# Attention on one core: weights left unnormalized, the reciprocal carried through a transpose into the output

## The chip, the cores and the metric

The kernel runs on one core of a Trainium2 chip. The metric is the device time of one execution in microseconds (us), the median of three runs. Engines are named as in the profile: PE (TensorE matmuls; PEld its weight loads), DVE (VectorE), ACT (ScalarE), POOL (GpSimd), SP (SyncE, which issues the DMAs; SPq is its queue).

## The reference

Rotary attention with 4 x 8 heads, 576 positions and a head size of 64, then two feed-forward layers over 2304 tokens (512 to 2048 to 512). All is float32 for the caller.

```python
q_rot, k_rot = rotate(q), rotate(k)                      # cos/sin tables
scores = matmul(q_rot, k_rot.T) / sqrt(64)
attn = exp(scores - max(scores))
attn = attn / (sum(attn) + 1e-9)
x = matmul(attn, v)                                      # (2304, 512) after the heads are joined
h = x @ w_in;  g = where(h > 0, h, exp(min(h, 0)) - 1);  x = g @ w_out      # layer 1
h = x @ w2_in; g = h - tanh(h);                          out = g @ w2_out   # layer 2
```

## The kernel before

**Attention.** Heads are worked in 16 pairs. The 576 queries of a pair are cut into five blocks; with both heads that makes nine items a pair: items 0 to 7 are four blocks of 128 queries for head 0 and head 1 in turn, item 8 holds the last 64 queries of both heads. One iteration of the loop at L377 is called a *round* here, and a round of a pair is numbered r = 0 to 8 like its item. In round i the kernel records, in this order:

- DMA loads (SP), then the row maximum of item i (`emit_max`, DVE, L216);
- `flush` (L256): the copies out of PSUM of what was transposed in the round before (two of five on DVE at L260, three on ACT at L262), and the attention output: ACT rounds it to the fp32r high part `xh` (L273), and one flush later DVE writes the low part `xl` (L265);
- the scores of item i+1 (`emit_s`, PE, L207), whose PSUM tile has two buffers, so that scores i+1 wait for the exponential of item i-1;
- the exponential of item i (ACT, L230), which also sums the row into `den`;
- `emit_norm` of the block that ended with item i-1: DVE adds 1e-9 to the two columns of sums (L242) and takes reciprocals (L243), POOL multiplies the 128x576 weights of each head by them in place (L246);
- a step of `prep` for a coming pair, by the table at L339 to L349: two multiplications by the cos/sin tables (POOL, L142), an addition (DVE, L144), the high part (ACT, L147), the low part `hl` (DVE, L152) and behind it, in `place`, the DMAs that put high and low part into the q tiles (L177) and k tiles (L174). For k these stand in r = 2, 3, 4 and the k tiles are first read by the scores of the next pair in r = 8;
- in the first sixteen pairs a fifth of the conversion of a layer-1 weight block from raw 64-bit words (`conv_w`; L78 and L79 on DVE in r = 5 of the even pairs);
- the transposes of item i-D with D = 4 (PE, L293; the 64 left-over columns of both heads together at L307), and the products with v (PE, L325) by the table PV_AT: for a group of 256 queries six matmuls in one round and four two rounds later, there with the ten of the last 64 queries in every second case; the trace shows a float32 product as two instructions.

**Layers.** Then come 192 steps of 24 or 21 matmuls each (L442, L498, L500), in which PE reads `xh` and `xl`; layer 1 sums into `acc`, and at its end `acc` is split into high and low part again (L522, L523).

The order on each engine is the order of recording (`manual_schedule`); engines run in order and wait on semaphores.

Of the kernel before, what the change touches and what calls it, by code (L numbers as in the profile page):

```python
# [23 lines left out]
def attention_elu_tanhshrink(ctx: ExitStack, tc: tile.TileContext, qk, v, w1i, w1o, w2i, w2o, tab, out):  # L24
# [76 lines left out]
    with ExitStack() as actx:  # L101
# [9 lines left out]
        ident = acst.tile([128, 128], F32, name="ident")  # L111
        tabs = acst.tile([128, 2, S], F32, name="tabs")
        zero = acst.tile([128, 64], F32, name="zero")
        qa_t = [acst.tile([128, 640], F32R, name=f"qa{i}") for i in range(2)]
# [4 lines left out]
        def load_qk(p, x):  # L119
            if p == 1 and x == 0:  # L120
                t = p3.tile([128, 2, S], F32, tag="a", name="t0")
            else:
                t = (p1, p2)[x].tile([128, 2, S], F32, tag=f"t{x}", name=f"t{x}")
            nc.sync.dma_start(out=t, in_=qk[p, :, 2 * x:2 * x + 2, :])
            t_t[p, x] = t
# [6 lines left out]
        def prep(p, x, i):  # L132
            t = t_t[p, x]
            mul = SCALE if p > 0 and x == 0 else 1.0
            if i < 2:
                if p == 0 and x == 0:
                    nc.vector.scalar_tensor_tensor(
                        out=t[:, i, :], in0=t[:, i, :], scalar=SCALE, in1=tabs[:, i, :], op0=ALU.mult, op1=ALU.mult
                    )
                else:  # L140
                    eng = nc.vector if p < 2 and i == 1 else nc.gpsimd
                    eng.tensor_tensor(out=t[:, i, :], in0=t[:, i, :], in1=tabs[:, i, :], op=ALU.mult)  # L142
            elif i == 2:
                nc.vector.tensor_tensor(out=t[:, 0, :], in0=t[:, 0, :], in1=t[:, 1, :], op=ALU.add)  # L144
            elif i == 3:
                hl_t[p, x] = p1.tile([128, 2, S], F32R, tag=f"hl{x}", name=f"hl{x}")
                nc.scalar.mul(hl_t[p, x][:, 0, :], t[:, 0, :], mul)  # L147
            else:
                hl = hl_t.pop((p, x))
                if p > 0:  # L150
                    t_t.pop((p, x))
                nc.vector.scalar_tensor_tensor(  # L152
                    out=hl[:, 1, :], in0=t[:, 0, :], scalar=mul, in1=hl[:, 0, :].bitcast(F32),
                    op0=ALU.mult, op1=ALU.subtract,
                )
# [78 lines left out]

        def emit_norm(i):
# [13 lines left out]

        ev = [0]  # L250
        late, late_x, late_l = [], [], []

# [3 lines left out]
        def flush():  # L256
# [6 lines left out]
            late.clear()  # L263
            for x0, hp, o, n in late_l:
                nc.vector.tensor_tensor(  # L265
                    out=xl[:, hp, x0:x0 + n], in0=o[:, 0:n], in1=xh[:, hp, x0:x0 + n].bitcast(F32),
                    op=ALU.subtract,
                )
            late_l.clear()
            for p, grp, o, n in late_x:  # L270
                b, hp = divmod(p, 4)
                x0 = b * S + 256 * grp
                nc.scalar.copy(out=xh[:, hp, x0:x0 + n], in_=o[:, 0:n])  # L273
                late_l.append((x0, hp, o, n))
            late_x.clear()

        def emit_t(i):
# [3 lines left out]
            if (u % 2 == 0) and h in (0, None):  # L281
                if grp < 2:
                    aT_t[p, grp] = (p2.tile([128, 2, 4, 256], F32, tag="aT", name="aT"),
                                    p2.tile([128, 256], F32, tag="aTr", name="aTr"))
                else:
                    aT_t[p, grp] = (p1.tile([128, 2, 4, 64], F32, tag="aT2", name="aT2"),
                                    p1.tile([128, 64], F32, tag="aTr2", name="aTr2"))
            aT, aTr = aT_t[p, grp]
# [5 lines left out]
            if h is None:  # L294
                for hh in range(2):
                    evac(aT[:, hh, :, 0:64], pt[:, :, 64 * hh:64 * hh + 64])
                pr = ps_t.tile([128, 4, 128], F32, tag="pt", name="pr")
                for hh in range(2):
                    sl = slice(64 * hh, 64 * hh + 64)
                    nc.tensor.matmul(out=pr[sl, 0, 0:64], lhsT=a[sl, 0, 512:576], rhs=ident[sl, sl],  # L300
                                     start=True, stop=True)
                evac(aTr[:, 0:64], pr[:, 0, 0:64])
                return
            evac(aT[:, h, :, q0:q0 + 128], pt)
            if h == 1:
                pr = ps_t.tile([128, 4, 128], F32, tag="pt", name="pr")
                nc.tensor.transpose(pr[:, 0, :], a.rearrange("p h s -> p (h s)")[:, 512:640], ident)  # L307
                evac(aTr[:, q0:q0 + 128], pr[:, 0, :])

        o_t = {}  # L310

        def emit_pv(p, grp, c):
# [6 lines left out]
            for h in range(2):  # L319
# [10 lines left out]
            if grp == 2:  # L330
                v_t.pop(p)
            late_x.append((p, grp, o, n))
# [6 lines left out]
        early = {1: ((None, 0, 0, 1, 2, 3), (None, 0, 0, 0, 1, 2)), 2: ((2, 4, 5, 7, 7, 8), (4, 7, 9, 11, 12, 13))}  # L339
        for p in range(1, NPAIR):  # L340
            i0 = NI * (p - 1)
            for x in range(2):
                when = [i0 + o for o in ((-8, -6, -4, -3, -2, -1), (-7, -2, 0, 2, 3, 4))[x]]
                if p in early:
# [6 lines left out]
        with tc.manual_schedule():  # L351
            for x in range(2):
                t = t_t[0, x] = (p1, p2)[x].tile([128, 2, S], F32, tag=f"t{x}", name=f"t{x}")
                for i in range(2):
# [3 lines left out]
            load_qk(1, 0)  # L358
            load_qk(1, 1)
            load_v(0)  # L360
            make_identity(nc, ident)
# [8 lines left out]
            n = len(items)  # L370
            pend = []
            emit_s(0)
            PV_AT = ((1, 1, 1, 3, 3), (1, 1, 1, 3, 3), (2, 2, 2, 2, 2))
# [3 lines left out]
            for i in range(n + D + 1):  # L377
                p, r = divmod(i, NI)
                for f, *arg in sched.get(i, ()):
                    if f is not prep:  # L380
                        f(*arg)
                if r == 0 and p % 2 == 0 and p // 2 < len(first_w):
                    load_w(first_w[p // 2])
                if i < n:
# [6 lines left out]
                if 0 <= i - 1 < n:  # L391
                    emit_norm(i - 1)
                if p < NPAIR:
# [19 lines left out]
            flush()  # L413


# [9 lines left out]

    acc = fcst.tile([128, KC * NTOK], F32, name="acc")
    b1 = fcst.tile([128, 1], F32, name="b1")
# [5 lines left out]
    def emit_f1(i):  # L433
# [4 lines left out]
        for c in range(KC):  # L438
            ws = slice(128 * c, 128 * c + 128)
            xs = slice(NB * t, NB * t + NB)  # L440
            for wp, x in ((0, xh), (0, xl), (1, xh)):
                nc.tensor.matmul(out=hp, lhsT=w[:, wp, ws], rhs=x[:, c, xs], start=(m == 0), stop=(m == 3 * KC - 1))  # L442
                m += 1
# [61 lines left out]
    def emit_acc():  # L505
        while y_done:
            l, g, t, ys = y_done.pop()
            for e, y in enumerate(ys):
# [11 lines left out]
                if l == 0:  # L520
                    xs = slice(NB * t, NB * t + NB)
                    nc.scalar.copy(out=xh[:, e, xs], in_=a)  # L522
                    nc.gpsimd.tensor_tensor(  # L523
                        out=xl[:, e, xs], in0=a, in1=xh[:, e, xs].bitcast(F32), op=ALU.subtract
                    )
                else:
# [6 lines left out]
    with tc.manual_schedule():  # L533
# [82 lines left out]
```

## Time and profile before

| | us |
|---|---|
| runs | 1137.78, 1138.52, 1139.23 (median 1138.52) |
| profiled execution, its own time | 1137.68 |
| its span | 1135.9 |
| attention (to the first unbroken run of layer-1 matmuls) | about 324.6 |
| layers | about 811 |

| engine | busy us | share |
|---|---|---|
| PE | 1100.1 | 97% |
| DVE | 769.7 | 68% |
| ACT | 689.3 | 61% |
| POOL | 647.6 | 57% |

The shares are means over two unlike stages. In the layers PE is busy all the time and the other engines are not; in attention DVE, POOL and PE are all busy. The granted clock of TensorE is at its full level in all 40 slices of the page, so the clock plays no part.

### The profile page before, as it was taken

The page shows a single profiled execution, that of the slowest core. Times are in us where ns is not written, and L with a number is a line of the kernel's source. Part 1 is how long each engine was busy: PE and PEld are TensorE (multiplying, and loading weights), DVE is VectorE, ACT ScalarE, POOL GpSimd, SP SyncE. Part 2 cuts the span into 40 slices and gives each one's busy share as a digit, 9 for nine tenths or more (in the row PEclk, how much of TensorE's full clock was granted, in tenths as well). Part 3 has the DMA queues.
Part 4 walks back from the last instruction along what each step waited for, and adds up shares of the span by engine and source line. Part 5 has one row for each costly group of instructions (what it writes and reads, how often), then busy time and mean ns, then how long its engine had stood idle before and what let it go on. Part 6 is the DMA issues. An engine that isn't in the chain of part 4 may idle for free.

```text
span 1135.9 us, 18496 instructions
## 1 busy us (share of the span) xinstructions
PE 1100.1 (97%) x6656; PEld 983.9 (87%) x6656; DVE 769.7 (68%) x1383; ACT 689.3 (61%) x1479; POOL 647.6 (57%) x585
## 2 busy tenths in 40 slices
PE   2899999999999999999999999999999999999998
PEld 1677777777789999999999999999999999999997
DVE  5998889888743434455445466677768777877665
ACT  3677777777634343333333344688888788877774
POOL 2877888778423333333333366676666666666443
PEclk9999999999999999999999999999999999999999
DMA  7767676766211111111111111111111111110102
GB/s 231 197 193 192 191 182 189 200 195 187 72 38 38 38 38 40 54 38 38 57 38 38 38 50 44 38 38 38 56 38 38 38 55 39 38 38 1 57 34 79
DMA packets 29627, 91.96 MB, mean 81 GB/s; under 512 B 4192, under 2 KB 4192, under 8 KB 29536
## 3 DMA queue, kind: packets, MB, share of 16 engines
q1 hardware_dynamic: 29536, 90.78, 27.8%
q8 instruction: 53, 0.87, 0.3%
q14 instruction: 38, 0.31, 0.1%
HBM read 57.74 MB, written 4.72 MB: 55 GB/s over the span
## 4 chain that ended last, share of the span: by engine, by line
PE 86%; DVE 10%; DMA 2%; ACT 1%; issue 1%; SPq 1%; DVEq 0%; ACTq 0%
PE h L442 36%; PE y L498 18%; PE y L500 18%; PE o L325 6%; PE s L207 5%; PE pt L293 3%; DVE nm L216 3%; DVE aT L260 2%; DVE hl L152 1%; DMA k<-hl 1%; DVE den L242 1%; DVE t L144 1%; DVE f L79 1%; PE pr L307 1%; DMA tabs<-in_tab 0%
## 5 line engine op out<-in xcount | busy, mean ns | idle before, releaser
L442 PE MATMUL h<-xh,w 128*128 128x384 f32 x1536 | 423.3, 336 | 0.0
L483 POOL TENSOR_TENSOR g<-f,g 128x384 fp32r<-128x384 f32 x192 | 214.9, 1120 | 232.5 <-ACT g L482 229.2
L442 PEld LDWEIGHTS h<-xh,w 128*128 128x128 f32 x1536 | 281.6, 188 | 3.8
L442 PE MATMUL h<-xl,w 128*128 128x384 f32 x768 | 258.3, 336 | 0.0
L498 PE MATMUL y<-g,w 128*128 128x384 f32 x1152 | 219.0, 339 | 0.0
L500 PE MATMUL y<-w,g 128*128 128x512 f32 x864 | 216.5, 395 | 0.0
L498 PEld LDWEIGHTS y<-g,w 128*128 128x128 f32 x1152 | 204.0, 188 | 0.0
L500 PEld LDWEIGHTS y<-w,g 128*128 128x128 f32 x864 | 161.6, 188 | 31.4
L246 POOL TENSOR_SCALAR a<-a,r 128x576 f32<-128x576 f32 x144 | 132.4, 932 | 70.5 <-DVE r L243 50.4
L459 POOL TENSOR_TENSOR w<-w,u 128x384 f32<-128x384 f32 x96 | 105.9, 1103 | 100.1 <-ACT w L458 100.1
L482 ACT CAST g<-f 128x384 fp32r<-128x384 f32 x192 | 97.9, 510 | 99.4 <-PE y L498 97.7
L442 PEld LDWEIGHTS h<-xl,w 128*128 128x128 f32 x768 | 144.2, 188 | 3.8
L470 DVE TENSOR_SCALAR f<-f 128x384 f32<-128x384 f32 x96 | 38.4, 400 | 153.9 <-ACT f L451 153.9
L451 ACT ACTIVATE f<-h 128x384 f32<-128x384 f32 x96 | 47.2, 492 | 150.0 <-PE h L442 146.4
L230 ACT ACTIVATE a<-s,nm 128x576 f32<-128x576 f32 x144 | 107.6, 747 | 39.6 <-DVE nm L216 31.7
L216 DVE TENSOR_REDUCE nm<-s 128x1 f32<-128x576 f32 x144 | 108.1, 751 | 32.4 <-PE s L207 31.6
L96 POOL TENSOR_TENSOR w<-f,w 128x512 fp32r<-128x512 f32 x64 | 82.7, 1292 | 54.2 <-ACT w L95 54.1
L517 DVE TENSOR_TENSOR acc<-y,acc 128x384 f32<-128x384 f32 (+1 forms) x126 | 74.0, 612 | 47.2 <-PE y L498 42.0
L474 DVE TENSOR_TENSOR f<-h,f 128x384 f32<-128x384 f32 x96 | 53.2, 554 | 71.4 <-ACT f L460 70.9
L476 DVE COPY_PREDICATED f<-mask,w 128x384 f32<-128x384 uint32 x96 | 91.7, 956 | 10.3 <-ACT g L482 0.5
L142 POOL TENSOR_TENSOR t<-t,tabs 128x576 f32<-128x576 f32 x59 | 88.1, 1494 | 15.6 <-DMA t<-in_qk 15.6
L293 PE MATMUL pt<-ident,a 128*128 128x128 f32 x576 | 89.0, 277 | 4.0 <-ACT aT L262 2.7
(58 smaller groups left out, 1479.5 us busy)
## 6 DMA issues: line engine op xcount, KB each, us to landing
k<-hl SPq DMA_DIRECT2D x64, 288.0 KB, 4.6
t<-in_qk SPq DMA_DIRECT2D x30, 576.0 KB, 4.8
raw<-in_w1i SPq DMA_DIRECT2D x16, 512.0 KB, 3.7
raw<-in_w1o SPq DMA_DIRECT2D x16, 512.0 KB, 3.7
raw<-in_w2i SPq DMA_DIRECT2D x16, 512.0 KB, 3.6
raw<-in_w2o SPq DMA_DIRECT2D x16, 512.0 KB, 3.6
v<-in_v SPq DMA_DIRECT2D x16, 288.0 KB, 5.1
qa<-hl SPq DMA_DIRECT2D x32, 144.0 KB, 2.3
```

Of the source, the lines that this page charges most:

```text
L142: eng.tensor_tensor(out=t[:, i, :], in0=t[:, i, :], in1=tabs[:, i, :], op=ALU.mult)
L216: nc.vector.tensor_reduce(out=nm, in_=s_t[i][:, :, 0:288], axis=AX.XY, op=ALU.max, negate=True)
L230: nc.scalar.activation(out=a.rearrange("p (x c) -> p x c", x=2), in_=s[:, :, 0:288], func=AF.Exp, bias=nm_t.pop(i), scale=1.0, accum_out=den,)
L246: nc.gpsimd.tensor_scalar(out=a, in0=a, scalar1=r[:, x:x + 1], scalar2=1.0, op0=ALU.mult, op1=ALU.mult)
L293: nc.tensor.transpose(pt[:, c, :], a[:, h or 0, c0:c0 + 128], ident)
L442: nc.tensor.matmul(out=hp, lhsT=w[:, wp, ws], rhs=x[:, c, xs], start=(m == 0), stop=(m == 3 * KC - 1))
L459: nc.gpsimd.tensor_tensor(out=w, in0=w, in1=u, op=ALU.mult)
L476: nc.vector.copy_predicated(f, mask.bitcast(U32), w)
L482: nc.scalar.copy(out=g[:, 0, :], in_=f)
L483: nc.gpsimd.tensor_tensor(out=g[:, 1, :], in0=f, in1=g[:, 0, :].bitcast(F32), op=ALU.subtract)
L498: nc.tensor.matmul(out=y_t[e][:, 0:NB], lhsT=w[:, wp, es], rhs=gt[:, gp, :], start=st, stop=sp)
L500: nc.tensor.matmul(out=y_t[e], lhsT=gt[:, gp, es], rhs=w[:, wp, :], start=st, stop=sp)
```

## The change

1. The weights stay unnormalized. `emit_norm` becomes `emit_recip`: the 1e-9 is added one column at a time (two 128x1 instructions in place of one 128x2), and POOL, in place of two 128x576 multiplications, spreads the two reciprocals over a 128x128 tile `rs` (64 columns each).
2. `rs` is transposed on PE into the same PSUM tile as the left-over columns (L312; for the 64-query block L305), and the copy out of PSUM takes both (256 columns for 128; 192 for 64).
3. The attention output is multiplied by it on DVE (`flush_o`, L277) into a float32 array `xa`; `xh`, `xl` and `acc` are gone. `flush_o` stands behind `emit_recip`.
4. `split_x` makes high and low part for layer 1 per tile of 384 tokens: tile 0 in the last eight rounds of attention, tiles 1 to 5 in the first 20 steps of layer 1 (ACT and POOL). `acc` of layer 1 is `xa`.
5. D is 3 instead of 4: all transposes and products stand one round earlier against the scores.
6. The scale of q goes into a table `tabq` (POOL, once); the low part of q and k for all pairs but the first moves from DVE to POOL (L158); the q load is issued two rounds earlier; the raw weight loads stand at other rounds.

```diff
+    def split_x(t, c):
+        a = xa[:, NTOK * c + NB * t:NTOK * c + NB * t + NB]
+        nc.scalar.copy(out=x[:, 0, c, :], in_=a)
+        nc.gpsimd.tensor_tensor(out=x[:, 1, c, :], in0=a, in1=x[:, 0, c, :].bitcast(F32), op=ALU.subtract)
...
-                nc.vector.scalar_tensor_tensor(
-                    out=hl[:, 1, :], in0=t[:, 0, :], scalar=mul, in1=hl[:, 0, :].bitcast(F32),
+                eng = nc.vector if p == 0 else nc.gpsimd
+                eng.tensor_tensor(
+                    out=hl[:, 1, :], in0=t[:, 0, :], in1=hl[:, 0, :].bitcast(F32), op=ALU.subtract
...
-            nc.vector.tensor_scalar_add(den, den, 1e-9)
+            for x in range(nh):
+                nc.vector.tensor_scalar_add(den[:, x:x + 1], den[:, x:x + 1], 1e-9)
             nc.vector.reciprocal(out=r[:, 0:nh], in_=den)
-            for x in range(nh):
-                a = a_t[p, u][:, x, :]
-                nc.gpsimd.tensor_scalar(
-                    out=a, in0=a, scalar1=r[:, x:x + 1], scalar2=1.0, op0=ALU.mult, op1=ALU.mult
-                )
+            nc.gpsimd.tensor_copy(
+                rs.rearrange("p (h d) -> p h d", h=nh), r[:, 0:nh].unsqueeze(2).broadcast_to([128, nh, 128 // nh])
+            )
...
+        def flush_o():
+            for p, grp, o, aTr, n in late_o:
...
+                    nc.vector.tensor_tensor(out=xa[sl, x0:x0 + n], in0=o[sl, 0:n], in1=r, op=ALU.mult)
...
+                nc.tensor.transpose(pr[:, 128:256], r_t.pop((p, u)), ident)
+                evac(aTr[:, :, q0:q0 + 128], pr[:, 0:256].rearrange("p (x c) -> p x c", x=2))
...
-        D = 4
+        D = 3
...
-                if r == 0 and p % 2 == 0 and p // 2 < len(first_w):
-                    load_w(first_w[p // 2])
+                if i == 1 or i % (2 * NI) == 12:
+                    load_w(first_w[nw.pop()]) if nw else None
...
-                    emit_norm(i - 1)
+                    emit_recip(i - 1)
+                flush_o()
...
+                if n - 8 <= i < n and (i - n) % 2 == 0:
+                    split_x(0, (i - n + 8) // 2)
...
+            if i < NJ * (NT - 1):
+                split_x(i // NJ + 1, i % NJ)
```

On PE, from the product rounds of one pair to the first scores of the next (s are scores, pt and pr transposes, o products with v), before:

```order
L307 MATMUL pr<-ident,a 128x128
L325 MATMUL o<-aT,v 64x256 x2
L325 MATMUL o<-aTr,v 64x256 x2
L325 MATMUL o<-aT_697,v 64x64 x8
L325 MATMUL o<-aTr_698,v 64x64 x2
L207 MATMUL s<-k_476,qb_98 128x288 x4
L293 MATMUL pt<-ident,a 128x128 x4
L207 MATMUL s<-k_473,qa_96 128x288 x4
L207 MATMUL s<-k_476,qb_98 128x288 x2
```

and after:

```order
L312 MATMUL pr<-ident,rs 128x128
L330 MATMUL o<-aT,v 64x256 x2
L330 MATMUL o<-aTr,v 64x256 x2
L330 MATMUL o<-aT_703,v 64x64 x8
L330 MATMUL o<-aTr_704,v 64x64 x2
L212 MATMUL s<-k_496,qa_97 128x288 x4
L296 MATMUL pt<-ident,a 128x128 x4
L212 MATMUL s<-k_499,qb_99 128x288 x4
L296 MATMUL pt<-ident,a 128x128 x4
L311 MATMUL pr<-ident,a 128x128
L312 MATMUL pr<-ident,rs 128x128
L212 MATMUL s<-k_496,qa_97 128x288 x4
```

The block of 14 products now stands before the scores of items 6, 7 and 8 of the pair, where it stood before those of 7 and 8; and there is one more transpose (of `rs`) behind each `pr`.

On DVE, rounds 3 to 6 of an even pair (nm is the maximum), before:

```order
L216 TENSOR_REDUCE nm<-s 128x1
L260 COPY aT_697<-pt 128x256
L242 TENSOR_SCALAR den<-den 128x2
L243 RECIPROCAL r<-den 128x2
L152 SCALAR_TENSOR_TENSOR hl_692<-t_393,hl_692 128x576
L216 TENSOR_REDUCE nm<-s 128x1
L260 COPY aT<-pt 128x4x128
L78 TENSOR_SCALAR f<-f 128x512
L79 TENSOR_SCALAR f<-f 128x512
L216 TENSOR_REDUCE nm<-s 128x1
```

and after:

```order
L221 TENSOR_REDUCE nm<-s 128x1
L266 COPY aT<-pt 128x4x128
L249 TENSOR_SCALAR den<-den 128x1 x2
L250 RECIPROCAL r<-den 128x2
L221 TENSOR_REDUCE nm<-s 128x1
L266 COPY aTr<-pr 128x2x128
L277 TENSOR_TENSOR xa<-o,aTr 128x256
L277 TENSOR_TENSOR xa<-o,aTr_704 64x64 x2
L85 TENSOR_SCALAR f<-f 128x512
L86 TENSOR_SCALAR f<-f 128x512
L221 TENSOR_REDUCE nm<-s 128x1
```

The subtraction `hl` has left DVE; the products of the block of 14 are multiplied there in round 5, ahead of the conversion (L85, L86) and of the maximum of item 6.

On POOL, rounds 2 to 8 of a pair, before:

```order
L246 TENSOR_SCALAR a<-a,r 128x576 x2
L142 TENSOR_TENSOR t_895<-t_895,tabs 128x576
L246 TENSOR_SCALAR a<-a,r 128x576 x2
L142 TENSOR_TENSOR t_895<-t_895,tabs 128x576
L246 TENSOR_SCALAR a<-a,r 128x576 x2
L142 TENSOR_TENSOR t_916<-t_916,tabs 128x576
```

and after:

```order
L251 COPY rs<-r 128x128
L147 TENSOR_TENSOR t_605<-t_605,tabq 128x576
L251 COPY rs<-r 128x128
L158 TENSOR_TENSOR hl_732<-t_413,hl_732 128x576
L147 TENSOR_TENSOR t_605<-t_605,tabq 128x576
L251 COPY rs<-r 128x128
L147 TENSOR_TENSOR t_682<-t_682,tabs 128x576
```

The low part of k (`hl_732`) stands on POOL in round 4, behind the spreading of the reciprocals of that round.

## Rows read from the trace of the kernel before

**Rows 1.** Windows (window, length, busy us of each engine (instructions), clock, DMA share, GB/s)
```profile
100.00:200.00 100.00, 96.86 (x796) 71.23 (x795) 92.14 (x187) 71.60 (x179) 80.87 (x74) 1.00 0.68 187
340.00:380.00 40.00, 40.00 (x229) 40.00 (x228) 14.46 (x31) 15.85 (x33) 15.06 (x14) 1.00 0.15 44
...
307.00:324.60 17.60, 16.89 (x155) 11.52 (x153) 7.48 (x20) 8.21 (x21) 3.81 (x6) 1.00 0.00 1
```

**Rows 2.** Chain that ended last, attention (start us, us, what)
```profile
161.50 2.04 PE o L325 x28
...
198.45 2.04 PE o L325 x28
```

**Rows 3.** The same chain, two pairs from 199 us on
```profile
211.31 0.60 DVE aT L260
...
212.24 0.66 DVE nm L216
...
214.07 0.76 DVE hl L152
...
216.48 1.50 DVE f L79
...
219.04 0.76 DVE t L144
```

**Rows 4.** Timeline of PE (start us, us, engine line op out<-in shapes [idle before])
```profile
210.35 0.60 PE L293 MATMUL pt<-ident,a 128*128 128x128 f32 x4
210.78 0.27 PE L307 MATMUL pr<-ident,a 128*128 128x128 f32 x1
...
212.42 1.52 PE L325 MATMUL o<-aT,v 128*64 128x256 f32 x12
213.87 0.80 PE L207 MATMUL s<-k,qb 128*128 128x288 f32 x4
214.50 0.60 PE L293 MATMUL pt<-ident,a 128*128 128x128 f32 x4
...
221.41 0.77 PE L207 MATMUL s<-k,qa 128*128 128x288 f32 x4
222.52 0.63 PE L293 MATMUL pt<-ident,a 128*128 128x128 f32 x4 [0.34 <-ACT aT L262]
...
233.94 0.60 PE L293 MATMUL pt<-ident,a 128*128 128x128 f32 x4
235.06 0.33 PE L307 MATMUL pr<-ident,a 128*128 128x128 f32 x1 [0.52 <-DVE aT L260]
```

**Rows 5.** Groups by line and shape, 100 to 300 us (count, busy us, mean ns, idle before)
```profile
L246 POOL TENSOR_SCALAR a<-a,r 128x576 f32<-128x576 f32 x98 | 91.5, 946 | 38.1 <-DVE r L243 20.4 <-PE s L207 8.5 <-ACT xh L273 2.5
L142 POOL TENSOR_TENSOR t<-t,tabs 128x576 f32<-128x576 f32 x40 | 59.5, 1487 | 5.3 <-DMA t<-in_qk 5.3
L242 DVE TENSOR_SCALAR den<-den 128x2 f32<-128x2 f32 x43 | 19.5, 454 | 0.0
L152 DVE SCALAR_TENSOR_TENSOR hl<-t,hl 128x576 fp32r<-128x576 f32 x21 | 15.9, 758 | 0.8
L265 DVE TENSOR_TENSOR xl<-o,xh 128x256 fp32r<-128x256 f32 x22 | 9.1, 415 | 0.0
L260 DVE COPY aTr<-pr 128x128 f32<-128x128 f32 x22 | 6.1, 278 | 0.0
L242 DVE TENSOR_SCALAR den<-den 128x1 f32<-128x1 f32 x11 | 1.6, 145 | 0.0
```

**Rows 6.** Timeline of POOL around the conversion of a weight block
```profile
216.13 1.56 POOL L142 TENSOR_TENSOR t<-t,tabs 128x576 f32<-128x576 f32 x1
```

**Rows 7.** SP's queue, and the landing of the k transfers
```profile
214.85 3.41 SPq L174 DMA_DIRECT2D k<-hl x4
```

**Rows 8.** Groups by line and shape, whole run: the split after layer 1
```profile
L523 POOL TENSOR_TENSOR xl<-acc,xh 128x384 fp32r<-128x384 f32 x24 | 27.1, 1157 | 7.0 <-ACT xh L522 7.0
```

More of the change, by code (lines that the diff above doesn't have):

```diff
@@ L112, in attention_elu_tanhshrink @@
         tabs = acst.tile([128, 2, S], F32, name="tabs")
+        tabq = acst.tile([128, 2, S], F32, name="tabq")
         zero = acst.tile([128, 64], F32, name="zero")
@@ L119, in load_qk @@
         def load_qk(p, x):
[L120 to L123, printed above, removed]
+            t = p2.tile([128, 2, S], F32, tag=f"t{x}", name=f"t{x}")
             nc.sync.dma_start(out=t, in_=qk[p, :, 2 * x:2 * x + 2, :])
@@ L133, in prep @@
             t = t_t[p, x]
-            mul = SCALE if p > 0 and x == 0 else 1.0
             if i < 2:
@@ L141, in prep @@
                     eng = nc.vector if p < 2 and i == 1 else nc.gpsimd
-                    eng.tensor_tensor(out=t[:, i, :], in0=t[:, i, :], in1=tabs[:, i, :], op=ALU.mult)
+                    tb = (tabq, tabs)[x]
+                    eng.tensor_tensor(out=t[:, i, :], in0=t[:, i, :], in1=tb[:, i, :], op=ALU.mult)
             elif i == 2:
@@ L146, in prep @@
                 hl_t[p, x] = p1.tile([128, 2, S], F32R, tag=f"hl{x}", name=f"hl{x}")
-                nc.scalar.mul(hl_t[p, x][:, 0, :], t[:, 0, :], mul)
+                nc.scalar.copy(out=hl_t[p, x][:, 0, :], in_=t[:, 0, :])
             else:
@@ L263, in flush @@
             late.clear()
[L264 to L270, printed above, removed]
-                b, hp = divmod(p, 4)
[L272 to L275, printed above, removed]
+        def flush_o():
+            for p, grp, o, aTr, n in late_o:
+                b, hp = divmod(p, 4)
+                x0 = NTOK * hp + b * S + 256 * grp
+                for sl, r in ((slice(0, 128), aTr[:, 1, :]),) if grp < 2 else (
+                        (slice(0, 64), aTr[0:64, 0, 64:128]), (slice(64, 128), aTr[64:128, 0, 128:192])):
+                    nc.vector.tensor_tensor(out=xa[sl, x0:x0 + n], in0=o[sl, 0:n], in1=r, op=ALU.mult)
+            late_o.clear()
         def emit_t(i):
@@ L296, in emit_t @@
                     evac(aT[:, hh, :, 0:64], pt[:, :, 64 * hh:64 * hh + 64])
-                pr = ps_t.tile([128, 4, 128], F32, tag="pt", name="pr")
+                pr = ps_t.tile([128, 512], F32, tag="pt", name="pr")
                 for hh in range(2):
                     sl = slice(64 * hh, 64 * hh + 64)
-                    nc.tensor.matmul(out=pr[sl, 0, 0:64], lhsT=a[sl, 0, 512:576], rhs=ident[sl, sl],
+                    nc.tensor.matmul(out=pr[sl, 0:64], lhsT=a[sl, 0, 512:576], rhs=ident[sl, sl],
                                      start=True, stop=True)
-                evac(aTr[:, 0:64], pr[:, 0, 0:64])
+                nc.tensor.transpose(pr[:, 64:192], r_t.pop((p, u)), ident)
+                evac(aTr[:, 0, :], pr[:, 0:192])
                 return
@@ L305, in emit_t @@
             if h == 1:
-                pr = ps_t.tile([128, 4, 128], F32, tag="pt", name="pr")
-                nc.tensor.transpose(pr[:, 0, :], a.rearrange("p h s -> p (h s)")[:, 512:640], ident)
-                evac(aTr[:, q0:q0 + 128], pr[:, 0, :])
+                pr = ps_t.tile([128, 512], F32, tag="pt", name="pr")
+                nc.tensor.transpose(pr[:, 0:128], a.rearrange("p h s -> p (h s)")[:, 512:640], ident)
+                nc.tensor.transpose(pr[:, 128:256], r_t.pop((p, u)), ident)
+                evac(aTr[:, :, q0:q0 + 128], pr[:, 0:256].rearrange("p (x c) -> p x c", x=2))
         o_t = {}
@@ L342, in attention_elu_tanhshrink @@
             for x in range(2):
-                when = [i0 + o for o in ((-8, -6, -4, -3, -2, -1), (-7, -2, 0, 2, 3, 4))[x]]
+                when = [i0 + o for o in ((-10, -6, -4, -3, -2, -1), (-7, -2, 0, 2, 3, 4))[x]]
                 if p in early:
@@ L352, in attention_elu_tanhshrink @@
             for x in range(2):
-                t = t_t[0, x] = (p1, p2)[x].tile([128, 2, S], F32, tag=f"t{x}", name=f"t{x}")
+                t = t_t[0, x] = p2.tile([128, 2, S], F32, tag=f"t{x}", name=f"t{x}")
                 for i in range(2):
@@ L359, in attention_elu_tanhshrink @@
             load_qk(1, 1)
+            nc.gpsimd.tensor_scalar(out=tabq, in0=tabs, scalar1=SCALE, scalar2=1.0, op0=ALU.mult, op1=ALU.mult)
             load_v(0)
@@ L371, in attention_elu_tanhshrink @@
             pend = []
+            nw = list(range(len(first_w)))[::-1]
             emit_s(0)
@@ L424, in attention_elu_tanhshrink @@
     ps_y = ctx.enter_context(tc.tile_pool(name="ps_y", bufs=4, space=PSUM))
-    acc = fcst.tile([128, KC * NTOK], F32, name="acc")
+    for t in range(1, NT):
+        x_t[t] = fcst.tile([128, 2, KC, NB], F32R, name=f"x{t}")
+    acc = xa
     b1 = fcst.tile([128, 1], F32, name="b1")
@@ L439, in emit_f1 @@
             ws = slice(128 * c, 128 * c + 128)
-            xs = slice(NB * t, NB * t + NB)
-            for wp, x in ((0, xh), (0, xl), (1, xh)):
-                nc.tensor.matmul(out=hp, lhsT=w[:, wp, ws], rhs=x[:, c, xs], start=(m == 0), stop=(m == 3 * KC - 1))
+            for wp, xp in ((0, 0), (0, 1), (1, 0)):
+                nc.tensor.matmul(
+                    out=hp, lhsT=w[:, wp, ws], rhs=x_t[t][:, xp, c, :], start=(m == 0), stop=(m == 3 * KC - 1)
+                )
                 m += 1
@@ L520, in emit_acc @@
                 if l == 0:
[L521 to L525, printed above, removed]
+                    split_x(t, e)
                 else:
```

24 lines of the change are left out of this document (13 added, 11 removed).

## The prediction, made before the changed kernel ran

> **What bounds the kernel now.** I read the windows by stage first. In the layers PE is busy for all of the time while DVE, ACT and POOL are at 36 to 40% [rows 1]: there, only a change in PE's own work or a late input can move the time, and the change leaves PE's matmuls as they are. In attention PE is at 97%, but DVE at 92% and POOL at 81% beside it [rows 1], so the share alone doesn't say which engine sets the pace. The chain of waits does. It passes the block of 14 products (28 instructions in the trace) of every second pair at 161.50 and 198.45 [rows 2]: two pairs take 36.95 us, 18.5 us a pair. Inside, the chain is on PE most of the time, and for some 10 us of the 37 on DVE, from the maximum of item 3 over the copies, `hl` of k, the slow L79 of the weight conversion and the addition [rows 3].
>
> How much of the 18.5 us PE waits is read from the spacing of its instructions. Four score matmuls take 0.63 us (213.87 to 214.50), four transposes 0.44 us (210.35 to 210.78), six products (12 in the trace) 1.45 us (212.42 to 213.87) [rows 4]. Where the spacing is longer, PE stood still: at 222.52 the transposes come 1.11 us after their scores, 0.48 late; at 235.06 the left-over transpose comes 1.12 us after the four, 0.68 late, because DVE had not yet emptied a PSUM tile [rows 4]. With smaller ones I put all such waits at 1.8 us in two pairs (an estimate). So PE has about 17.6 us of work a pair and 0.9 us of waiting: 14.4 us over 16 pairs is all that a relief of DVE and POOL can bring in attention.
>
> **What the change costs and gives.**
>
> *PE's added work.* Each of the 80 blocks gets one more 128x128 transpose. Four take 0.44 us, so one takes 0.11 and 80 take 8.8 us. Nothing hides it: PE is the engine that is nearest to full, and it runs in order. Bounds: 0.11 to 0.14 us each (the four at 214.50 and at 222.52 are spaced a little wider), 9 to 11 us. I take 9.
>
> *What leaves the other engines.* POOL loses two 946 ns multiplications in each full block and one in a short one, 144 x 0.946 = 136 us, and gains 80 spreads of 128x128 and 30 `hl` subtractions. The spread isn't in the trace: nearest is L246 itself, at most 0.95, scaled by columns 0.2; I take 0.3. The subtraction is like L142, 1.49 us. That is 24 + 45 = 69 us gained, a net relief of 67 us [rows 5]. DVE loses 30 subtractions of 0.76 (23 us) and, for the sums, 64 x (0.454 - 2 x 0.145) = 10 us; it gains wider copies (32 of 0.278 that become about 0.415, the price of L265, which also reads 256 columns from PSUM: 4 us) and 16 more 64-column multiplications (3 us); the multiplication by the reciprocal itself costs what L265 cost [rows 5]. Net about 26 us, 1.6 a pair, and DVE falls from 92% to some 84%. ACT loses the casts to `xh`. All three were near, but not over, the pace of PE, so this counts only through the 14.4 us of waits.
>
> *Where PE will wait after it.* Here the round order matters more than the sums. With D = 3 the block of 14 products (2.04 us, rows 2) stands in round 4 and the six of each group in rounds 2 and 7, in which item 8's long scores stand too.
>
> (a) Rounds 5 to 7 of the eight even pairs. Call T the end of the block of 14. Scores 6 follow at T, scores 7 with six transposes end by T + 2.5, then scores 8 want the exponential of item 6. DVE can't multiply the products before T: that ends at T + 0.5. Only then do the conversion's two instructions come; the second took 1.50 us in before [rows 3], as long as POOL's multiplication beside it ran (216.13 to 217.69, rows 6), and POOL now starts such a multiplication in the same place, since `hl` of k holds it until then. So the maximum of item 6 ends near T + 2.5, the exponential (0.8 us) near T + 3.4, and scores 8 are about 0.95 late. In before the block of 14 lay beside the conversion and hid it.
>
> (b) Rounds 1 to 4 of each pair. From the scores of item 2: maximum 0.8 + 0.66, copy 0.60, sums and reciprocals about 0.55, addition 0.76, maximum 0.66, half copy 0.33, ACT's two copies and the exponential about 1.4: 5.8 us until scores 5 may start [durations of rows 3 and 5]. PE's own work between them is about 5.3. Late by 0.5.
>
> (c) Round 0 waits 0.2 us for a copy; and k arrives later. In before SP starts k's transfers at 214.85, has issued the four at 218.3, and the last lands about 4.5 us after its issue, some 222.5 [rows 7]; its scores stand at about 224.5 (222.52 and then 0.55 + 1.45). Now `hl` of k runs 1.49 on POOL for 0.76 on DVE and behind the spread, and the rounds between are 2 us shorter, since one product group has moved ahead of them: the 2 us of slack are gone, a wait of 0.1 or so in odd pairs.
>
> Two pairs: 0.95 + 2 x 0.5 + 2 x 0.2 + 0.1 = 2.45 us, against 1.8 now; eight times the difference is +5.2 us. Since I took every tie at its late end I count half, +2.6. Bounds: all waits gone, -14.4; (a) at 1.8 and (c) at 0.7 in each pair, +16.
>
> *Port sharing.* L79 above shows that a DVE instruction stands until POOL's is through: 1.50 us for an instruction that ends 0.3 after POOL does [rows 3, 6]. The Trainium skill ("SBUF — State Buffer", Who interferes with whom) says that tensor_scalar in a two-port mode, and two-input operations from SBUF, share an exclusive port pair with GpSimd and block for the whole instruction, while operations with one SBUF input don't. The trace agrees. By that rule the new multiplication (one input in PSUM) and the one-column sums escape, which speaks for the change, but the conversion in (a) does not; without the rule (a) would be 0.4 instead of 0.95, 8 x 0.55 = 4.4 us less.
>
> *Splits.* 24 pairs of ACT and POOL instructions of 1.16 us [rows 8] on POOL: four in the last rounds of attention, where POOL has no rotations left, twenty in the first twenty layer steps, one per 4.2 us step with POOL at 38% [rows 1]. Hidden by PE's matmuls; without that cover up to 1.2 us each. I count nothing.
>
> *Ends.* One round fewer lies behind the last scores, and the last blocks don't wait for POOL; but in the tail of before PE already works 16.9 of 17.6 us [rows 1], so this saves at most 0.7 there and a round of transposes that fit into PE's idle start, together 2 us. `tabq` puts one to two L246 times, about 1.5 us, on POOL ahead of the first rotation of k: 0 to +1.5. I take -1.5 in all (-3 to +1.5).
>
> **Sum.** 9 + 2.6 - 1.5 = +10.1. On the profiled execution's own 1137.68 that is 1147.8; the median of the runs is 0.8 above it: 1148.6.
>
> **Rivals.**
>
> *R1, faster: DVE's and POOL's relief removes PE's waits.* For it: the chain lies on DVE for about a quarter of a pair, and the 0.68 us wait came from a DVE copy behind a sum of two columns that stood for POOL, which is what the one-column form avoids. Against it: (a) and (b) rest on the order of rounds and not on DVE's load. If waits fall to 0.1 a pair: 9 - 12.8 - 2.5 = -6, 1132. It decides below 0.25 us of waiting a pair.
>
> *R2, slower: POOL's queue and k.* `hl` of both q and k stands in one in-order queue with the rotations and the spreads; if the spread costs 0.95, or the k transfers land at the late end (6.8, rows 7), scores of the next pair wait in every pair, 0.7 us more: 9 + 16 = +25, 1163. It decides if the k transfers start over 1 us later against the scores than now. Against it: POOL has spare time in round 3.
>
> *R3, a draw.* The waits fall to half (7.2 us) and the ends give 2: 9 - 7.2 - 2 = 0, 1138.
>
> *R4, the layers.* If the splits delay the `g` low parts, layer 1 pays up to 20 x 1.2 = 24 us. Against it: four steps lie between split and use. Chance below 0.02, inside R2's.
>
> **How the numbers follow.** Forecast (waits as they are or a little worse, added transposes in full, 1142 to 1157): 0.48. R1: 0.27. R2: 0.13. R3: 0.12. A difference within 0.2% (2.3 us) is what a measurement of this kernel can't tell from none. Slower is forecast and R2, 0.61; faster is R1, 0.27; the same is R3, 0.12. Range: R1's centre to the forecast's upper end, 1132 to 1158, with about 0.1 beyond each side; the forecast alone spans 1142 to 1157.
>
> **What the changed profile would show.** 80 transposes of `rs` at 0.11 us spacing on PE. DVE at some 84% and POOL near 65% between 100 and 300 us, with the end of attention later all the same. In even pairs a PE gap ahead of the second half of round 7, with L85, L86 and the maximum ahead of it in the chain. A chain with k's transfers in every pair would mean R2; an attention stage that ends before 324 us, with two pairs under 36.9 us, R1, and that PE's waits came from DVE's load and POOL's blocking after all. Layers longer than 811 us would contradict the part on the splits.

## The result, and the profile after

The changed kernel takes 1150.18 us (median of 4 runs, 1148.77 to 1150.95), against 1138.54 for the kernel before (1137.78 to 1139.23): ratio 1.0101, 95% interval 1.0083 to 1.0118, slower by 11.6 us. The forecast was 1148.6. The profiled execution took 1148.77 us with a span of 1147.0; for before the two were 1137.68 and 1135.9.

Two rows of the page, busy time by engine and the chain of waits by engine:

```profile
PE 1109.8 (97%) x6736; PEld 993.4 (87%) x6736; DVE 749.9 (65%) x1433; ACT 687.0 (60%) x1455; POOL 615.7 (54%) x576
...
PE 94%; DVE 2%; ACT 2%; DMA 1%; SPq 0%; POOL 0%; issue 0%; ACTq 0%; POOLq 0%
```

The chain has left DVE: it was on PE for 86% of the span before and on DVE for 10%, and is now 94% and 2%. The windows of attention and of the layers (columns as in [rows 1]):

```profile
100.00:200.00 100.00, 95.89 (x782) 71.58 (x783) 77.43 (x195) 64.49 (x155) 56.92 (x60) 1.00 0.69 185
200.00:300.00 100.00, 97.10 (x791) 72.00 (x787) 75.10 (x192) 65.63 (x158) 57.43 (x61) 1.00 0.64 167
335.69:1147.00 811.31, 807.56 (x4318) 768.36 (x4314) 507.34 (x835) 482.21 (x966) 438.93 (x388) 1.00 0.14 42
```

and of the layers before:

```profile
324.57:1135.90 811.33, 807.56 (x4318) 768.20 (x4314) 498.02 (x835) 474.04 (x947) 418.07 (x368) 1.00 0.14 42
```

Between 100 and 200 us DVE fell from 92% to 77% and POOL from 81% to 57% [rows 1], more than was forecast, and PE is about as full as it was (96% for 97%). The layers begin where the first unbroken run of layer 1 stands in PE's timeline, 335.69, 11.1 us later than in before (324.57), and take 811.3 us, as in before. The whole loss is in attention. The chain there, whose blocks of 14 products answer to [rows 2]:

```profile
88.16 2.04 PE o L330 x28
...
203.83 2.04 PE o L330 x28
...
222.60 2.04 PE o L330 x28
...
242.26 2.04 PE o L330 x28
...
280.70 2.04 PE o L330 x28
```

Now every pair shows its block, so the chain runs along PE in all of them. The two pairs from 203.83 take 38.43 us against 36.95, +1.48; eight times that is 11.8, a little more than the 11.1 that the stage lost. Of the two, the pair from 203.83 takes 18.77 and the one from 222.60 takes 19.66. PE's timeline shows what parts them; its rows are the scores of item 8, ahead of which (a) of the prediction puts a wait, of the odd pair (208.44) and of the even one (228.11). Between them stand scores 2 (215.45) and scores 5 (221.05), of which (b) speaks, and the added transposes, in a short block of 64 queries (L305) and in a full block (L312):

```profile
208.44 0.80 PE L212 MATMUL s<-k,qa 128*128 128x288 f32 x4 [0.23 <-ACT a L235]
...
215.45 0.79 PE L212 MATMUL s<-k,qa 128*128 128x288 f32 x4
...
218.21 0.33 PE L305 MATMUL pr<-ident,rs 128*128 128x128 f32 x1
218.47 1.52 PE L330 MATMUL o<-aT,v 128*64 128x256 f32 x12
...
220.56 0.60 PE L296 MATMUL pt<-ident,a 128*128 128x128 f32 x4
221.05 0.79 PE L212 MATMUL s<-k,qb 128*128 128x288 f32 x4
...
226.61 0.27 PE L311 MATMUL pr<-ident,a 128*128 128x128 f32 x1
226.72 0.27 PE L312 MATMUL pr<-ident,rs 128*128 128x128 f32 x1
228.11 0.80 PE L212 MATMUL s<-k,qa 128*128 128x288 f32 x4 [1.12 <-ACT a L235]
```

In the full blocks the transposes of `rs` stand 0.11 us behind those of `a`, as priced. In the short block the transpose of `rs` delays the products behind it by 0.26 us (218.21 to 218.47), which the prediction had not priced. The even pair waits 1.12, the odd one 0.23: the difference, 0.89, is the difference of the two pairs. The chain ahead of 228.11 passes DVE's maximum and ACT's exponential, as forecast:

```profile
226.37 0.76 DVE nm L221
...
227.22 0.84 ACT a L235 x2
...
228.11 1.43 PE s L212 x10
```

What DVE and POOL did before that maximum (timelines of the two engines):

```profile
223.81 0.42 DVE L277 TENSOR_TENSOR xa<-o,aTr 128x256 f32<-128x256 f32 x1 [0.40 <-PE o L330]
224.69 0.46 DVE L277 TENSOR_TENSOR xa<-o,aTr 64x64 f32<-64x64 f32 x2 [0.45 <-PE o L330]
225.18 0.70 DVE L85 TENSOR_SCALAR f<-f 128x512 f32<-128x512 f32 x1
225.91 0.43 DVE L86 TENSOR_SCALAR f<-f 128x512 uint32<-128x512 uint32 x1
```
```profile
222.81 1.41 POOL L158 TENSOR_TENSOR hl<-t,hl 128x576 fp32r<-128x576 f32 x1
224.19 1.41 POOL L147 TENSOR_TENSOR t<-t,tabq 128x576 f32<-128x576 f32 x1
```

DVE stands twice for the block on PE, then makes the conversion's two instructions, and only then reads the scores. POOL is through at 225.60; L85 lost 0.27 to it (0.70 instead of 0.43, the time of L86), and L86 lost nothing, where 1.5 had been forecast.

The waits of PE in 100 to 300 us, before and then after (us in all, times, longest), complete the picture:

```profile
PE pr L307 <- DVE aT L260: 2.7, 6, 0.5
...
PE pt L293 <- ACT aT L262: 1.7, 5, 0.4
```
```profile
PE s L212 <- ACT a L235: 6.7, 10, 1.1
```

PE no longer waits for the copies on DVE and ACT; it waits for exponentials instead. Neither list has a wait for k's transfers.

### The profile page after: what moved, and what is told of

Read it like the earlier page. It is cut to its first block, busy times and chain, and to the rows that moved or that the text cites. A ratio compares the mean times of both kernels' runs of the same rounds, so it can differ in the third digit from the quotient of the medians.

```text
span 1147.0 us, 18545 instructions
## 1 busy us (share of the span) xinstructions
PE 1109.8 (97%) x6736; PEld 993.4 (87%) x6736; DVE 749.9 (65%) x1433; ACT 687.0 (60%) x1455; POOL 615.7 (54%) x576
## 4 chain that ended last, share of the span: by engine, by line
PE 94%; DVE 2%; ACT 2%; DMA 1%; SPq 0%; POOL 0%; issue 0%; ACTq 0%; POOLq 0%
PE h L453 35%; PE y L511 18%; PE y L513 17%; PE s L212 9%; PE o L330 8%; PE pt L296 5%; ACT a L235 1%; DVE nm L221 1%; PE pr L311 1%; PE pr L312 0%; DMA tabs<-in_tab 0%; DMA k<-hl 0%; PE pr L303 0%; PE pr L305 0%; ACT aT L268 0%
## 5 line engine op out<-in xcount | busy, mean ns | idle before, releaser
L453 PE MATMUL h<-x,w 128*128 128x384 f32 x2304 | 434.3, 337 | 0.0
L453 PEld LDWEIGHTS h<-x,w 128*128 128x128 f32 x2304 | 407.1, 188 | 7.6
L251 POOL COPY rs<-r 128x128 f32<-128x128 f32 x80 | 36.7, 459 | 132.6 <-DVE r L250 75.9
L530 DVE TENSOR_TENSOR xa<-y,xa 128x384 f32<-128x384 f32 (+1 forms) x126 | 73.9, 612 | 47.2 <-PE y L511 42.0
L469 ACT ACTIVATE u<-h 128x384 f32<-128x384 f32 x96 | 47.2, 492 | 68.4 <-PE h L453 54.2
L268 ACT COPY aT<-pt 128x512 f32<-128x512 f32 x96 | 52.8, 550 | 51.5 <-PE pt L296 30.5
L330 PE MATMUL o<-aT,v 128*64 128x256 f32 (+1 forms) x768 | 80.2, 337 | 0.0
```

Of the source, the lines that this page charges most:

```text
L453: nc.tensor.matmul(out=hp, lhsT=w[:, wp, ws], rhs=x_t[t][:, xp, c, :], start=(m == 0), stop=(m == 3 * KC - 1))
```

## The experiments

The reasons to be tested: PE's transposes are the loss (theory), or the new order of the rounds and POOL's queue are (rival). Eleven kernels ran, in three groups; within a group they share the runs of before (1138.76, 1138.31 and 1139.24 us). Below, "two pairs" is the mean of five such stretches in the chain of blocks (for the changed kernel (280.70 - 88.16) / 5), and "waits" is PE waiting for exponentials between 100 and 300 us. Differences to the changed kernel are those of the medians; by the ratios they come out up to 0.6 us smaller or larger. Differences to the kernel before are to the median of before in the same group.

| kernel | us | ratio to before, 95% | two pairs | waits |
|---|---|---|---|---|
| before | 1138.54 | 1 | 36.96 | none listed |
| after | 1150.18 | 1.0101 (1.0083 to 1.0118) | 38.51 | 6.7 |
| e1 no transposes | 1140.80 | 1.0017 (1.0008 to 1.0025) | 37.45 | 9.9 |
| e2 transposes doubled | 1156.64 | 1.0156 (1.0142 to 1.0170) | 39.32 | 4.6 |
| e3 conversion first | 1153.58 | 1.0128 (1.0114 to 1.0142) | 38.93 | 8.8 |
| e4 lag 4 | 1153.15 | 1.0124 (1.0108 to 1.0139) | – | 4.5 |
| e5 conversion later | 1148.33 | 1.0090 (1.0077 to 1.0103) | 38.29 | 3.7 |
| e6 low part on DVE | 1146.94 | 1.0076 (1.0064 to 1.0088) | 38.22 | 5.3 |
| e7 before, one-column sums | 1135.75 | 0.9980 (0.9971 to 0.9989) | 36.75 | 0.2 |
| e8 before, lag 3 | 1144.37 | 1.0051 (1.0039 to 1.0063) | 38.42 | 6.1 |
| e9 = e1 and e6 | 1137.11 | 0.9985 (0.9977 to 0.9994) | 37.01 | 9.4 |
| e10 = e5 and e6 | 1145.34 | 1.0056 (1.0042 to 1.0070) | 38.21 | 3.7 |
| e11 = e7 and e5's move | 1135.13 | 0.9969 (0.9959 to 0.9978) | 36.48 | none listed |

**e1, no transposes of `rs`.**

```
-                nc.tensor.transpose(pr[:, 128:256], r_t.pop((p, u)), ident)
-                evac(aTr[:, :, q0:q0 + 128], pr[:, 0:256].rearrange(...))
+                evac(aTr[:, 0, q0:q0 + 128], pr[:, 0:128])
```

The same in the short blocks; the products are multiplied by `tabs`, and the copies out of PSUM have their old width again, so that this run takes away the wider copies too.

> The changed kernel without the 80 transposes of rs and with the copies out of PSUM at their old widths; the output is multiplied by a table instead of the reciprocals (so the weights stay unnormalized in the result), and the spread on POOL stays. Theory (the loss is PE's added work, which nothing hides): 80 x 0.11 to 0.15 us less, 9 to 12 us, so 1138 to 1141. Rival (PE waits anyway, the loss is in the new waits of DVE and POOL): at most 3 us less, 1147 to 1150.

Measured: 1140.80, 9.4 us less than the changed kernel. Theory holds. The wait of the even pairs stays, with nothing of the transposes in it (PE's timeline):

```profile
222.85 0.27 PE L310 MATMUL pr<-ident,a 128*128 128x128 f32 x1
224.18 0.80 PE L212 MATMUL s<-k,qa 128*128 128x288 f32 x4 [1.06 <-ACT a L235]
```

**e2, each transpose of `rs` twice**, the second into columns of `pr` that nothing reads.

```
+                nc.tensor.transpose(pr[:, 256:384], r_t.pop((p, u)), ident)
```

> The changed kernel with each transpose of rs done twice (the second copy is read by nobody); copies as wide as before. Theory: the price of 80 transposes by themselves, 80 x 0.11 to 0.15 us more, 9 to 12 us, so 1159 to 1162. Rival (transposes fit into waits): at most 3 us more, 1150 to 1153.

Measured: +6.5 us on the changed kernel, 0.08 each, between the two sides named (9 to 12, and at most 3). On PE the second stands 0.11 behind the first, but where PE would wait anyway it is free: the even pair's wait is 0.92 instead of 1.12, and the waits sum to 4.6 instead of 6.7.

```profile
232.99 0.27 PE L313 MATMUL pr<-ident,rs 128*128 128x128 f32 x1
233.10 0.27 PE L314 MATMUL pr<-ident,rs 128*128 128x128 f32 x1
234.29 0.80 PE L212 MATMUL s<-k,qa 128*128 128x288 f32 x4 [0.92 <-ACT a L235]
```

The two runs put a transpose at 0.08 to 0.12 us of time: its time on PE less what falls into a wait.

**e3, the conversion before the products' multiplication**, to take the wait of (a) away.

```
+                <the conversion's step, as it was behind the prep loop>
                 flush_o()
                 if p < NPAIR:
```

> The changed kernel with the step of the weight conversion recorded ahead of flush_o and not behind it, so that in round 5 of the even pairs DVE converts while PE is still in the block of 14 products. Theory: the wait of scores 8 in even pairs (1.12 us in the changed kernel's timeline of PE, against 0.23 in odd ones) falls to about 0.3, 8 x 0.8 = 6 us less: 1143 to 1146. Rival (scores 8 wait for item 6 by the order of rounds alone, whatever DVE does between): no change, 1149 to 1151.

Measured: +3.4 us, where -4 to -7 was expected. The theory of this run falls. DVE and POOL around that place:

```profile
227.42 1.17 DVE L85 TENSOR_SCALAR f<-f 128x512 f32<-128x512 f32 x1
228.63 1.53 DVE L86 TENSOR_SCALAR f<-f 128x512 uint32<-128x512 uint32 x1
```
```profile
226.90 1.41 POOL L158 TENSOR_TENSOR hl<-t,hl 128x576 fp32r<-128x576 f32 x1
228.27 1.60 POOL L147 TENSOR_TENSOR t<-t,tabq 128x576 f32<-128x576 f32 x1
```

The earlier conversion meets both of POOL's instructions, and each half ends 0.3 us after one of them (228.59 after 228.31, 230.16 after 229.87): 2.70 us for 0.86 of work. In the changed kernel DVE's standing for PE lets POOL run ahead; here that time is spent held by POOL, and the wait of scores 8 in the even pair grows to 1.52.

**e4, D = 4 in the changed kernel.**

```
-        D = 3
+        D = 4
```

> The changed kernel with D = 4, as before the change: transposes and products stand one round later against the scores. Theory: the block of 14 products covers the conversion again, and the wait of scores 8 is gone in all pairs (8 x 1.35 = 11 us), but DVE's copies get late for the left-over transposes as in before (1.2 us in two pairs, 10 us there, perhaps half of it with DVE relieved): 5 us less, 1141 to 1149. Rival (one round more behind the last scores and nothing else): 1 to 2 us more.

Measured: +3.0 us (the intervals overlap a little), where a gain was expected. The wait of (a) goes, but PE then waits 3.4 us in 200 for copies on DVE (`pr` <- `aT`), and once in two pairs some 0.9 us ahead of scores 0 of the next pair. DVE, POOL, ACT and PE at that place:

```profile
230.12 1.68 DVE L149 TENSOR_TENSOR t<-t 128x576 f32<-128x576 f32 x1
```
```profile
229.77 1.42 POOL L147 TENSOR_TENSOR t<-t,tabs 128x576 f32<-128x576 f32 x1
```
```profile
232.62 0.74 ACT L235 ACTIVATE a<-s,nm 128x576 f32<-128x576 f32 x1 [1.24 <-DVE nm L221]
```
```profile
233.51 0.80 PE L212 MATMUL s<-k,qa 128*128 128x288 f32 x4 [0.87 <-ACT a L235]
```

The addition L149 begins while POOL multiplies and takes 1.68 us for its usual 0.76; the maximum behind it is late by that, the exponential waits for the maximum, and scores 0 for the exponential. Over 100 to 300 us L149 takes 1.15 us in the mean (0.76 in the changed kernel). So the moved rounds put another DVE instruction beside POOL. The chain of this run also lists a transfer of k at this place, which landed at 233.28; but the exponential had started at 232.62, so it did not wait for it. Rival R2 is not seen here.

**e5, the conversion two rounds later.**

```
-                    c = NI * (p % 2) + r - 3
+                    c = NI * (p % 2) + r - 5
```

> The changed kernel with all five parts of the weight conversion two rounds later, so that its two DVE instructions stand in round 7 of the even pairs (beside item 8's scores and six products, 3.2 us of PE work) and not in round 5. Theory (the wait of scores 8 in even pairs is the conversion between the products' multiplication and the maximum of item 6): that wait falls from 1.4 us of spacing to the odd pairs' 0.5, 8 x 0.9 = 7 us less, 1142 to 1145. Rival (the order of rounds alone makes scores 8 late): no change, 1149 to 1151.

Measured: 1148.33, 1.9 us less, with overlapping intervals, and in neither range named. The waits nearly halve, and that of scores 8 in the even pair falls to the odd pair's 0.22, as the theory has it; but they spread over 15 places instead of 10. Of the 7 us that this wait was to give, 1.9 are left; where the rest returns was not read.

```profile
PE s L212 <- ACT a L235: 3.7, 15, 0.3
```

**e6, the low part of q and k on DVE**, as in before.

```
-                eng = nc.vector if p == 0 else nc.gpsimd
-                eng.tensor_tensor(
+                nc.vector.tensor_tensor(
```

> The changed kernel with the low part of q and k back on DVE for all pairs. Theory (DVE has time to spare, POOL's part is off the path): 0 to 3 us more, 1150 to 1153. Rival (POOL's slower subtraction and its place ahead of the rotation that blocks DVE cost time): 3 to 8 us less, 1142 to 1147.

Measured: 1146.94, 3.2 us less, though DVE gets 30 instructions of 0.76 us back. The rival holds. By the ratios it is 2.9, and the intervals meet at their ends; but the same edit gives 3.6 by the ratios between e1 and e9 and 3.9 between e5 and e10, where they lie apart. The even pair shows how (PE, DVE and POOL; lines past the edit are one lower):

```profile
225.12 0.80 PE L211 MATMUL s<-k,qa 128*128 128x288 f32 x4 [0.84 <-ACT a L234]
```
```profile
222.46 0.43 DVE L85 TENSOR_SCALAR f<-f 128x512 f32<-128x512 f32 x1
```
```profile
220.63 1.40 POOL L147 TENSOR_TENSOR t<-t,tabq 128x576 f32<-128x576 f32 x1
```

POOL's multiplication starts without `hl` ahead of it and is through at 222.03, before L85. L85 takes 0.43 instead of 0.70, and the wait falls by 0.28, from 1.12 to 0.84. Eight times that is 2.2 of the 3.2 us.

**e7 and e8, two parts of the change alone in the kernel before:** the 1e-9 added column by column (e7), and D = 3 (e8).

```
-            nc.vector.tensor_scalar_add(den, den, 1e-9)
+            for x in range(nh):
+                nc.vector.tensor_scalar_add(den[:, x:x + 1], den[:, x:x + 1], 1e-9)
```

> The kernel before with nothing changed but the 1e-9 added one column at a time. Theory (part of PE's 0.9 us of waiting a pair came from the two-column sum that stood on DVE while POOL multiplied, 0.45 us on average for 0.16 alone): 2 to 6 us less than before, 1133 to 1137. Rival (DVE's waits there are hidden): within 1 us of before, 1138 to 1139.

> The kernel before with D = 3 and nothing else. Theory (the lag by itself brings the wait of scores 8 in even pairs, because the block of 14 products no longer covers the conversion, but takes away the waits for DVE's copies): between 3 us less and 4 us more, 1136 to 1143. Rival (the lag of 3 is the loss): 8 to 12 us more, 1147 to 1151.

Measured: e7 1135.75, 2.6 us faster than before, with the whole interval below 1, as its theory has it. The sums in 100 to 300 us, to set beside those of [rows 5], and what PE still waits for the copy:

```profile
L243 DVE TENSOR_SCALAR den<-den 128x1 f32<-128x1 f32 x99 | 10.5, 143 | 0.0
```
```profile
PE pr L308 <- DVE aT L261: 1.0, 2, 0.6
```

The two-column form took 454 ns, one column takes 143, and the wait for the copy falls from 2.7 to 1.0 us in 200. e8 costs 6.1 us (5.8 by the ratio), which lies between its theory (at most 4 more) and its rival (at least 8). PE's waits for exponentials, and the scores of item 8 in an even pair:

```profile
PE s L207 <- ACT a L230: 6.1, 10, 1.7
```
```profile
224.95 0.80 PE L207 MATMUL s<-k,qa 128*128 128x288 f32 x4 [0.72 <-ACT a L230]
```

So the wait for exponentials comes with the lag of three rounds and not with the transposes; the kernel before has it too when its rounds are moved so. Its price in e8 is not the price in the changed kernel: in e8 the chain also passes POOL's multiplication of the weights (L246, 1.22 us at 228.96) ahead of a transpose, which the changed kernel doesn't have.

**e9, e1 and e6 together.**

> The changed kernel without the 80 transposes of rs (the products are multiplied by the table tabs instead, so the output isn't the reference's), and with the low part of q and k subtracted on DVE as in the kernel before. Theory: the transposes (9.4 us) and POOL's subtraction of the low parts (2.9 us) are separate costs that add: 1150.2 - 9.4 - 2.9 = 1137.9, so 1136 to 1139, no slower than the kernel before. Rival: both are ways of making PE wait less in the same place, or DVE has no room for 30 more instructions once PE is quicker: 1140 to 1143.

Measured: 1137.11. Theory holds: the transposes and POOL's subtraction add, and without them the rest of the change is not slower than before (ratio 0.9977 to 0.9994), lag of three included. Like e1, it has the narrower copies and leaves out the right factor of the products.

**e10, e5 and e6 together.**

> The changed kernel, all transposes kept, with the low part of q and k on DVE (alone -2.9 us) and each conversion step two rounds later (alone -1.2 to -1.9). Theory: PE's added work is a floor; what remains are some 1.9 us of waits in two pairs, so the two add at most to -4.5: 1145 to 1147, still over the kernel before. Rival: the added transposes are not a floor and the waits go: below 1142.

Measured: 1145.34, as the theory has it. With the transposes kept, the two edits give 4.8 us back, not the 11.6. The two kernels with `hl` on DVE that differ in the transposes and the width of their copies, e6 and e9, lie 9.8 us apart, near the 9.4 of e1.

**e11, e7 and the conversion two rounds later**, in the kernel before.

> The kernel before with the 1e-9 added column by column (alone 0.998 of it, 2.3 to 2.8 us) and each conversion step two rounds later. Theory: in the kernel before, L79 of the conversion stands 1.5 us beside POOL's multiplication and lies on the chain of every second pair; two rounds later it meets another rotation or normalization, so it gains 0 to 3 us more: 1133 to 1136. Rival: the conversion two rounds later stands before the maxima that gate the next pair, as it did in the changed kernel, and costs 1 to 4 us: 1137 to 1140.

Measured: 1135.13, ratio 0.9969, the lowest median of all and ahead of both kernels by 4.1 and some 15 us. That the later conversion adds to e7 is not settled: the intervals overlap (0.9959 to 0.9978 and 0.9971 to 0.9989).

## Why the prediction was right

Measured +11.6, forecast +10.1. By its steps:

- **PE's transposes, +9.** Right in mechanism, too small in size. In the 64 full blocks a transpose of `rs` takes 0.11 us on PE, but in the 16 short ones 0.26: 64 x 0.11 + 16 x 0.26 = 11.2, where the working had 80 x 0.11 = 8.8 and at most 11. (Of the two rows named for 0.14 only the four at 222.52 are spaced wider.) "Nothing hides it" does not hold in full either: e1 gives 9.4 back, and there PE's waits grow from 6.7 to 9.9; e2 adds 6.5 for 80 more of 0.11, and the waits shrink to 4.6.
- **Waits and ends, +2.6 and -1.5.** By the means of five stretches two pairs grew by 1.55 us (36.96 to 38.51). The transposes are 8 x 0.11 + 2 x 0.26 = 1.40 of that, so the rest, the waits above all, grew by 0.15, which is 1.2 us in eight such stretches and not 2.6. Eight times 1.55 is 12.4, and the stage ends 11.1 later, so the ends gave 1.3. The stage's sum is then 11.2 + 1.2 - 1.3 = 11.1, where the forecast had 9 + 2.6 - 1.5 = 10.1: the first term was too small by about 2 and the second too large by about 1.4, and that the total came so near is in part luck. Counting half of the computed 5.2 was a guess; even the half was too much. The upper bound of +16 doesn't follow from its own terms, which give 8 x (1.8 + 1.0 + 0.4 + 1.4 - 1.8) = 22. e1, which has the rest of the change but not the wider copies, is 2.0 us above before (+1.1 forecast for waits and ends).
- **(a), scores 8 of even pairs.** Place and size were right, 1.12 against 0.95, and its cause in the lag is shown by e8, where D = 3 alone brings it (0.72). The step "the second took 1.50 us in before, and POOL now starts such a multiplication in the same place" failed: POOL's multiplication is over at 225.60, 0.3 us before L86 begins; L86 takes 0.43, and only L85 lost 0.27. So POOL's share of this wait, put at 0.55, was half of that: where L85 is free (e6) the wait is 0.84, 0.28 less. The rest of the time is that of the chain itself, block, multiplication, conversion, maximum and exponential. That the wait could be taken away for its full price was a further guess of mine, and e3, e4 and e5 speak against it: e3 makes it longer, e4 and e5 remove it or nearly so and pay elsewhere.
- **(b), 0.5 us in rounds 1 to 4.** This step failed. Scores 5 at 221.05 follow the start of the four transposes ahead of them by 0.49 us, where four take 0.44: 0.05 late. The exponential of item 3, which they wait for, ends at 220.99 (ACT's timeline):

```profile
220.78 0.21 ACT L235 ACTIVATION_READ_ACCUMULATOR a<-s,nm 128x1 f32 x1
```

From scores 2 (215.45) that is 5.54 us, where the walk over DVE and ACT had 5.8; and PE's own work between took 5.55 (5.60 to scores 5, less the 0.05), where the working had 5.3, in part because the short block's transpose takes 0.26. Each side was off by a quarter of a microsecond, and the wait was their difference.
- **(c), k's transfers.** Not seen: the list of waits has none in the changed kernel or in e4, and a single one of 0.3 us in e5. The 0.2 in round 0 is not in the list of the changed kernel either.
- **What leaves the other engines.** DVE came to 77% (84% forecast) and POOL to 57% (65%). In attention DVE lost 29 us of work and POOL 53 (busy time of the page less that of the layers), where 26 and 67 had been counted. POOL's spread takes 0.46 us in the mean (0.3 taken). What I gave no price is the move of `hl` to POOL: I counted 23 us as DVE's relief, and e6 shows that it costs 3.2, some 2.2 of it because it holds POOL's next multiplication against the conversion.
- **Splits and layers, nothing.** 811.3 us before and after.
- **What bound the kernel before.** The chain of before was on DVE for 15.7 of the 36.9 us of two pairs, not for some 10: the reading left out the odd pair's stretch, 6.1 us that end with the late left-over transpose at 235.06. In it lies a sum of two columns that took 1.19 us:

```profile
231.56 1.19 DVE den L242
```

R1 was wrong in size and right in mechanism: the two-column sum that stands for POOL does make PE wait, and e7 gets 2.6 us from it alone, not 12.8. The waits that the relief removed (`pr` <- `aT`, `pt` <- `aT`) are gone from the changed kernel too, and the waits of lag 3 came in their place. What stays open is how the 2.0 us of e1 split between the lag (6.1 in e8, POOL's multiplication of the weights included) and the gains against it, and what the wider copies cost alone; no run has the changed kernel with a lag of 4 and the rounds of everything else fitted to it.

The conversion's L85 shows how POOL holds DVE: it took 0.43, 0.70 and 1.17 us (e6, the changed kernel, e3) where POOL's instruction beside it ended before L85 began, 0.42 us after that and 0.89 us after that. Held, it ended 0.28 us after POOL's each time. The Trainium skill ("SBUF — State Buffer", Who interferes with whom) has such an instruction blocked until GpSimd's is through; the traces agree. It also lets an operation with one SBUF input, outside the two-port modes, through, and the multiplication L277, with its other input in PSUM, took 0.42 at 223.81 with POOL busy beside it.

## What to carry to other kernels

When the chain of waits and the busy shares disagree, price what the change adds on the fullest engine first: 80 transposes, 11 us on PE, outweighed 29 us taken off DVE and 53 off POOL, because the relief could only buy back waits. Price an instruction in each place where it will stand: the same transpose took 0.11 us in one and 0.26 in another. A wait found by walking the rounds is real, but it belongs to the order and not to the instruction that stands last in it: test by moving that instruction before counting its removal as a gain. A small sum over two columns that stands while GpSimd multiplies (454 ns in the mean, 143 for one column) is worth splitting by itself: e7 gained 0.2%.

## What the runs showed of the hardware that I had not expected

The spread on POOL is held too, not only DVE (group of the whole run, and two of its instructions):

```profile
L251 POOL COPY rs<-r 128x128 f32<-128x128 f32 x80 | 36.7, 459 | 132.6 <-DVE r L250 75.9
```
```profile
222.56 0.29 POOL L251 COPY rs<-r 128x128 f32<-128x128 f32 x1 [2.41 <-PE pr L311]
...
227.59 0.69 POOL L251 COPY rs<-r 128x128 f32<-128x128 f32 x1 [1.99 <-DVE r L250]
```
```profile
222.35 0.74 DVE L221 TENSOR_REDUCE nm<-s 128x1 f32<-128x576 f32 x1
...
227.37 0.75 DVE L149 TENSOR_TENSOR t<-t 128x576 f32<-128x576 f32 x1
```

The first runs beside a maximum that reads PSUM, and takes 0.29. The second runs beside DVE's addition of two SBUF halves (L149, 227.37 to 228.12), ends 0.16 us after it, and takes 0.69. With `hl` back on DVE the mean of the spread between 100 and 300 us is 0.68 to 0.70 (e6, e9; 0.48 in the changed kernel), and the kernel is faster all the same.
